# Delta-rule attention and a PReLU feed-forward on one core: order of transposes, fillers, copies and conversions around the opening

## The chip, the cores and the metric

The kernel runs on one core of a Trainium2 chip. The core has five engines that each work through their own instructions in order: TensorE (PE, matrix products, with a separate row PEld for loading the stationary operand), VectorE (DVE), ScalarE (ACT), GpSimd (POOL) and SyncE (SP, which here issues nearly all transfers). They wait for each other through semaphores. Products land in PSUM, from which DVE and ACT read. TensorE's clock is granted by a throttle, and the profile lists what was granted (1.00 is full speed, 0.50 half). The metric is the device time of one execution in microseconds, as a median over runs.

## What is computed

```python
# attention: batch 4, heads 8, 768 tokens, head dimension 48
k_n = k / (norm(k) + 1e-6)
for t in range(S):
    y[:, :, t] = einsum('bhd,bhde->bhe', q[:, :, t], state)
    v_old = einsum('bhde,bhd->bhe', state, k_n[:, :, t])
    state = state + beta[t] * einsum('bhd,bhe->bhde', k_n[:, :, t], v[:, :, t] - v_old)
x = y.transpose(0, 2, 1, 3).reshape(3072, 384)
# feed-forward: 384 -> 2048 -> 384
h = x @ w_in
g = maximum(h, 0) + alpha * minimum(h, 0)
out = g @ w_out
```

Everything is float32. A token's state depends on all tokens before it; within a chunk of tokens this dependence is a triangular system that can be solved at once.

## The kernel before

**Tiling.** The sequence is cut into 12 chunks of C = 64 tokens. A step `n` is one chunk for two of the four batches, so there are 24 steps; the partitions hold two times 64 tokens. In each step the inverse of a 64x64 triangular matrix per head is wanted. It is put together from 32x32 blocks (HB = 32): the two diagonal blocks are inverted, and the block between them follows from products (`between_1`, `between_2`).

**Inverting the diagonal blocks.** `grams(n)` multiplies keys with keys on PE, and DVE writes the scaled products to `same` (first columns) and `right` (second columns). `keep(n)` (line 424) copies the second half's own blocks, of 32 partitions and 256 elements each, from `right` to `same`: two copies a step, by DVE for n < 4 and t = 0 (line 430), otherwise by ACT (line 432). Four steps (NJ = 4) make one group m. After the fourth, DVE transposes the group to `block` (`turn_in`, 32x32 stream transposes, line 444), so that 128 blocks lie one in each partition. `eliminate(m)` inverts them there by 30 rounds of a product and a sum (lines 468 and 474). `back(m)` (line 480) transposes the result to two tiles, `turned` and `inverse`, in PIECES = 4 instructions each, first all of `turned`, then all of `inverse`. For the first group this takes too long, so `eliminate_small(0)` inverts only 16x16 blocks (14 rounds) and also ends in `back`; `cross` (line 527) joins them on PE: it multiplies `edge` with the first 16 rows or columns of `turned` (line 533), ACT copies the product to `half_way` (line 537), PE multiplies this with `inverse` (lines 542 and 548), and DVE adds it to `turned` (line 554) and `inverse` (line 556). These are 32x32x16 products.

**The opening.** The order of all instructions is written out by hand; an engine's instructions run in the order in which the code emits them. The first steps 0 and 1 are computed by `first_chunk` (line 1036). `place(i, (x,))` lets ACT copy parts of `turned` and `inverse` to `diag` and `inv` (line 579). `scale_v` scales v on DVE (line 643). `solve`, `outputs`, `next_state` and `to_ffn` are the products with the inverse (671), with the query products (684), for the new state (700), and transposes of the result (713); ACT copies the outputs to `y` (689) and to `xt` (715). `queries` (line 1017) multiplies the keys and queries of steps 0 and 1 ahead of time into a PSUM tile; its `mask(n)` lets DVE multiply them with a triangular mask into `a_t` (line 1029). `busy(n)` (line 967) issues `n` products of 128x128 with 128x512 whose result nobody reads: fillers (line 972).

**PSUM.** A tile `p_big` has two banks of 512 numbers a partition, and three buffers used in rotation; `ps_one` takes the first bank of one. Two more banks, `ffn_banks`, are used in turn by `ps_ffn`. The query products lie in a `p_big`, the fillers go to `ffn_banks`.

**Weights.** Both weight matrices are converted piece by piece (`weights`): a transfer brings a piece to a staging place, `begin` runs two ACT instructions on it (lines 205 and 206), and `finish`, a generator of two parts for each piece, runs two on DVE (lines 215 and 220), then lets SP fetch a further piece to the place that has come free (line 189). `part(gen, n)` takes n parts of a generator. w_in has 12 pieces and 6 places; its places lie in the tile of w_out. `begin_in(n)` makes sure that ACT has begun n pieces. `convert(n)` in `first_chunk` takes n parts of w_in's conversion; all in all it takes n = 14. w_out has 16 pieces (32 parts) and 7 places.

**The weaves.** `weave(*gens)` interleaves generators in proportion to the counts given with them. Four stages follow the opening:

- weave B: the second half of `cross(0)`, steps 2 and 3 (`ready`, `pair`), the rest of w_in's conversion with 10 parts of w_out's, `grams` of steps 4 to 7 (`statics`), and `ffn_in(0)`, the first product of the feed-forward for chunk 0 (PE line 802, ACT line 812, DVE line 814);
- weave C: the rest of w_out's conversion (22 parts), `ffn_in(1)`, `grams` of steps 8 and 9, and the first 12 parts of `eliminate(1)`;
- weave D: the other parts of `eliminate(1)` and `ffn_out(0)`, the second product (line 844), in which f runs over w_out's 16 row blocks, two products for each;
- after it, weave by weave, steps 4 to 23 with the feed-forward of the chunks before them.

Of the kernel before, what the change touches and what calls it, by code (L numbers as in the profile page):

```python
# [28 lines left out]
ALU = mybir.AluOpType  # L29
# [12 lines left out]
def kernel(  # L42
# [29 lines left out]
    def ps_big():  # L72


        return psum.tile([128, 2, 512], FP32, name="p_big", tag="big", bufs=3)
# [7 lines left out]
    def ps_ffn():  # L83
        turn[0] ^= 1
        return ffn_banks[turn[0]]

    def half(i):
        return slice(64 * i, 64 * i + 64)

    def dims(i):  # L90
        return slice(64 * i, 64 * i + D)
# [332 lines left out]
    def keep(n):  # L424

        m, j = n // NJ, n % NJ
        for t in range(2):
            own = slice(64 * t + HB, 64 * t + C)
            if n < NJ and t == 0:
                nc.vector.tensor_copy(out=same[m][own, j], in_=right[n % EARLY][own, 1:])  # L430
            else:
                nc.scalar.copy(same[m][own, j], right[n % EARLY][own, 1:])  # L432
        if j == NJ - 1 and m <= 2:
            for _ in turn_in(m):
                pass
# [3 lines left out]
    def turns(dst, src):  # L439


        n = HB // PIECES
        for i in range(PIECES):
            nc.vector.transpose(dst(slice(n * i, n * i + n)), src(slice(n * i, n * i + n)))  # L444
            yield
# [10 lines left out]
    def eliminate(m):  # L456

        if m > 2:
            yield from turn_in(m)
        r = block[m]  # L460
        nc.vector.tensor_tensor(out=r, in0=r, in1=inside, op=ALU.mult)
        nc.vector.memset(r.rearrange("p r c -> p (r c)")[:, :: HB + 1], 1.0)
        yield
        for j in range(1, HB - 1):
            n = HB - 1 - j
            prod = work.tile([128, HB * HB // 4], FP32, name="prod", bufs=2)
            prod = prod[:, 0 : j * n].rearrange("p (c i) -> p c i", c=j)
            nc.vector.tensor_tensor(  # L468
                out=prod,
                in0=r[:, 0:j, j : j + 1].to_broadcast([128, j, n]),  # L470
                in1=r[:, j : j + 1, j + 1 : HB].to_broadcast([128, j, n]),
                op=ALU.mult,
            )
            nc.vector.tensor_tensor(  # L474
                out=r[:, 0:j, j + 1 : HB], in0=r[:, 0:j, j + 1 : HB], in1=prod, op=ALU.add
            )
            yield
        yield from back(m)

    def back(m):  # L480
        r = block[m]
        turned[m] = work.tile([128, NJ * H, HB], FP32, name="turned", bufs=1)
        yield from turns(
            lambda x: turned[m][:, :, x].rearrange("c b r -> c r b"), lambda x: r[:, x]
        )
        inverse[m] = work.tile([128, NJ * H, HB], FP32, name="inverse", bufs=1)
        yield from turns(
            lambda x: inverse[m][:, :, x].rearrange("r b c -> r c b"),
            lambda x: r[:, :, x].rearrange("b r c -> b c r"),
        )  # L490

    WHOLE = HB - 1 + 2 * PIECES

# [2 lines left out]
    def eliminate_small(m):  # L496
        x = small[m]
        nc.vector.tensor_tensor(out=x, in0=x, in1=own_blocks(inside_), op=ALU.mult)
        nc.vector.memset(block[m][:, 0:LB, LB:HB], 0.0)
        nc.vector.memset(block[m][:, LB:HB, 0:LB], 0.0)  # L500
        nc.vector.memset(block[m].rearrange("p r c -> p (r c)")[:, :: HB + 1], 1.0)
        yield
        for j in range(1, LB - 1):
            n = LB - 1 - j
            prod = work.tile([128, HB * HB // 4], FP32, name="prod", bufs=2)
            prod = prod[:, 0 : 2 * j * n].rearrange("p (s c i) -> p s c i", s=2, c=j)
            nc.vector.tensor_tensor(
                out=prod,
                in0=x[:, :, 0:j, j : j + 1].to_broadcast([128, 2, j, n]),
                in1=x[:, :, j : j + 1, j + 1 : LB].to_broadcast([128, 2, j, n]),  # L510
                op=ALU.mult,
            )
            nc.vector.tensor_tensor(
                out=x[:, :, 0:j, j + 1 : LB], in0=x[:, :, 0:j, j + 1 : LB], in1=prod, op=ALU.add
            )
            yield
        yield from back(m)

    def edges(m, dst):

# [119 lines left out]
    def scale_v(n):  # L640
        if n < N and n not in nv:
            nv[n] = v_raw.pop(n)
            nc.vector.tensor_tensor(
                out=nv[n], in0=nv[n],
                in1=stats[n][0][:, :, None].to_broadcast([128, H, D]), op=ALU.mult,
            )
# [185 lines left out]
    def ffn_out(c, together=False):  # L832

        gs = gss.pop(c)
        p_o = {}
        if together:
            order = [(u, f) for f in range(FT) for u in range(2)]
        else:
            order = [(u, f) for u in range(2) for f in range(FT)]
        for u, f in order:  # L840
            assert len(out_done) > f
            if f == 0:
                p_o[u] = ps_ffn()[:, 0:DM]
            nc.tensor.matmul(  # L844
                p_o[u], gs[f // 2][:, f % 2, u * 128 : (u + 1) * 128], w_out[:, f],
                start=(f == 0), stop=(f == FT - 1),
            )
            if f == FT - 1:
                o_sb = work.tile([128, DM], FP32, name="o_sb")
                nc.scalar.copy(o_sb, p_o[u])  # L850
                store(c, u, o_sb)
            yield
# [67 lines left out]
    def part(gen, n):  # L920
        for _ in range(n):
            next(gen, None)
            yield

    def weave(*gens):

        live = [[0.0, i, 1.0 / n, g] for i, (g, n) in enumerate(gens)]
        while live:
            live.sort(key=lambda x: (x[0], x[1]))
            at = live[0]  # L930
            at[0] += at[2]
            try:
                next(at[3])
            except StopIteration:
                live.pop(0)
# [30 lines left out]

    def busy(n):

        if n > 0:
            p = ps_ffn()  # L970
            for _ in range(n):
                nc.tensor.matmul(p, ident, k_t[NJ - 1].rearrange("p g i -> p (g i)"))

    def pair(n):

# [40 lines left out]

    def queries():

        p = ps_big().rearrange("p a (n g i) -> p a n g i", n=2, g=G)
        for n in range(2):  # L1020
            for g, a, t in quarters():
                nc.tensor.matmul(
                    p[half(t ^ a), a, n, g], k_t[n][dims(a), g, half(t)],
                    q_t[n][dims(a), g, half(t)],
                )
            a_t[n] = work.tile([128, H, C], FP32, name="a_t")

        def mask(n):
            nc.vector.tensor_tensor(
                out=a_t[n].rearrange("p (a g) i -> p a g i", a=2), in0=p[:, :, n],  # L1030
                in1=minus[:, None, None, :].to_broadcast([128, 2, G, C]), op=ALU.mult,
            )

        return mask

    def first_chunk(mask, convert):

        both = (0, 1)
        middle = cross(0, slice(0, 2 * H), edge, half_way)
        next(middle)  # L1040
        busy(1)
        for i in both:
            mask(i)
        begin_in(6)
        convert(2)
        next(middle)
        busy(1)
        for i in both:
            place(i, (0,))
            scale_v(i)  # L1050
        for i in both:
            between_1(i)
            place(i, (1,))
        convert(4)
        busy(1)
        for i in both:
            place(i, (2,))
            between_2(i)
        begin_in(8)
        for i in both:  # L1060
            through_state(i)
        solve(0)
        convert(1)
        solve(1)
        convert(1)
        busy(1)
        for i in both:
            outputs(i)
            next_state(i)
            convert(2)  # L1070
            load_late(i + 2)
            load_v(i + 3)
        busy(1)
        for i in both:
            to_ffn(i)
        convert(2)
# [74 lines left out]
    begin_in(4)  # L1151
    for _ in eliminate_small(0):
        pass
    n = 14

    def convert(n):
        for _ in part(conv_in, n):
            pass
# [8 lines left out]
        (statics(NJ, 2 * NJ - 1), 2 * NJ + 1), (ffn_in(0), IN_PARTS),  # L1167
    )
    fetch_out(len(stages))
    blocks, SOON = eliminate(1), 12  # L1170
    weave(
        (conv_out, PARTS_OUT - 10), (ffn_in(1), IN_PARTS),
        (statics(2 * NJ, FIRST + 3), 2 * (FIRST + 4 - 2 * NJ) + 1), (part(blocks, SOON), SOON),
    )
    flips(FIRST + NJ, NJ)
# [1 line left out]
    prep(FIRST + NJ)  # L1177
    load_early(FIRST + NJ + NKE)
    load_q(NJ + 2)
    weave((part(blocks, WHOLE - SOON), WHOLE - SOON), (ffn_out(0, True), OUT_PARTS))  # L1180

    def prelude(n):
        place(n)
# [83 lines left out]
```

## Time and profile before

| | |
|---|---|
| median of 7 runs | 697.67 us (692.77 to 699.21) |
| the profiled execution | 696.54 us, its span 694.5 us |
| mean granted clock of PE | 0.988 |
| busy: PE, DVE, ACT | 671.5, 447.4, 253.0 us |
| weave B (54.1 to 102.0), busy PE / DVE / ACT | 46.19 / 30.90 / 31.55 of 47.9 us |
| weave C (102 to 134), busy PE / DVE / ACT | 26.13 / 26.14 / 20.67 of 32 us |
| weave D (134 to 154), busy PE / DVE / ACT | 20.00 / 17.47 / 0.89 of 20 us |
| from 200 us to the end, busy PE | 489.75 of 494 us |
| filler product, L972 | 26 records of two a product, 0.43 us apart at full clock |
| copy of own blocks by DVE (L430), by ACT (L432) | 0.28, 0.40 us |

How to read it: a time in the timeline counts from the first instruction of the span. A product in float32 leaves two records on PE. "L802" is line 802. In brackets behind an instruction stands the idle time of its engine before it, and the engine and line that ended it. The profiled execution is one of several; its clock, and with it its time, is its own.

### The profile page before, as it was taken

Reading aid. Unit: us, or ns where it says so; the run is one execution under the profiler, and the core shown is the slowest. Engines: PE = TensorE matmul, PEld = TensorE weight load, DVE = VectorE, ACT = ScalarE, POOL = GpSimd, SP = SyncE. Lnnn points to the kernel's source line nnn. Section 1 sums busy time; section 2 is a strip of 40 time slices with the busy share of each in tenths; the row PEclk is TensorE's granted clock in tenths of the full one; section 3 lists DMA queues with packets and bytes.
Section 4 is the critical chain, followed back from the end, with each engine's and each line's share of the span. In section 5 each row is a group of like instructions: output and inputs, shape, how many; then the busy total and the mean of one; then the engine's idle time right before and its main releaser. Section 6 shows DMA issues by size and latency. Waiting matters only on the chain.

```text
span 694.5 us, 22886 instructions
## 1 busy us (share of the span) xinstructions
PE 671.5 (97%) x10057; PEld 580.8 (84%) x10057; DVE 447.4 (64%) x1094; ACT 253.0 (36%) x603; POOL 19.5 (3%) x74
## 2 busy tenths in 40 slices
PE   6999998799999999999999999999999999999997
PEld 4577877556678998998998988988988989989997
DVE  5945778887898548957558967458867245245151
ACT  5836766415453243244243244124034034131020
POOL 4000001000000000000000000000000000000000
PEclk9969999999999999999999999999999999999999
DMA  8857653301322022022021111101111201100000
GB/s 130 221 145 183 156 114 111 76 10 40 62 57 48 13 59 48 13 59 47 14 59 37 35 26 36 37 24 36 36 27 35 47 21 30 33 4 2 24 1 23
DMA packets 110963, 37.76 MB, mean 54 GB/s; under 512 B 104160, under 2 KB 107248, under 8 KB 110864
## 3 DMA queue, kind: packets, MB, share of 16 engines
q1 hardware_dynamic: 109088, 35.81, 23.7%
q8 instruction: 79, 1.29, 0.8%
q10 hardware_dynamic: 1776, 0.49, 0.4%
q14 instruction: 20, 0.16, 0.1%
HBM read 31.56 MB, written 4.72 MB: 52 GB/s over the span
## 4 chain that ended last, share of the span: by engine, by line
PE 82%; DVE 9%; ACT 4%; DMA 2%; issue 1%; SPq 0%; ACTq 0%; DVEq 0%
PE p_ffn L802 32%; PE p_ffn L866 27%; PE p_ffn L844 4%; PE p_big L657 3%; PE p_big L384 3%; PE p_big L351 2%; PE p_big L614 2%; PE p_big L629 2%; PE p_big L671 2%; PE p_big L684 2%; PE p_big L700 1%; DVE prod L468 1%; DVE block L474 1%; DVE block L444 1%; PE p_big L713 1%
## 5 line engine op out<-in xcount | busy, mean ns | idle before, releaser
L802 PE MATMUL p_ffn<-xt,w_in 128*128 128x256 f32 x1152 | 268.8, 386 | 5.7 <-DVE sums L814 3.3
L802 PEld LDWEIGHTS p_ffn<-xt,w_in 128*128 128x128 f32 x1152 | 213.8, 191 | 36.9 <-ACT w_out L205 3.0
L814 DVE SCALAR_TENSOR_TENSOR act<-act,al_t,p_ffn 128x256 f32<-128x256 f32 x176 | 76.5, 476 | 71.7 <-ACT act L812 70.6
L812 ACT ACTIVATE act<-p_ffn 128x512 f32<-128x512 f32 x88 | 52.3, 594 | 120.4 <-PE p_ffn L802 120.3
L866 PE MATMUL p_ffn<-w_out,act 128*128 128x192 f32 x480 | 83.7, 328 | 0.0
L866 PEld LDWEIGHTS p_ffn<-w_out,act 128*128 128x128 f32 x480 | 78.6, 190 | 0.9
L474 DVE TENSOR_TENSOR block<-block,prod 128x30 f32<-128x30 f32 (+9 forms) x150 | 49.8, 332 | 5.2
L468 DVE TENSOR_TENSOR prod<-block 128x30 f32<-128x30 f32 (+9 forms) x150 | 48.8, 325 | 2.2
L886 DVE TENSOR_TENSOR o_sb<-u,p_ffn 128x192 f32<-128x192 f32 x40 | 13.3, 352 | 42.1 <-PE p_ffn L866 35.9
L373 ACT COPY q_t<-p_big 128x512 f32<-128x512 f32 x24 | 13.9, 590 | 58.0 <-PE p_big L351 58.0
L432 ACT COPY same<-right 32x256 f32<-32x256 f32 x44 | 17.7, 402 | 47.6 <-DVE right L393 47.4
L665 ACT COPY y<-p_big 128x384 f32<-128x384 f32 x22 | 10.5, 478 | 66.3 <-DVE r L660 66.3
L373 ACT COPY k_t<-p_big 128x512 f32<-128x512 f32 x24 | 13.9, 579 | 54.7 <-PE p_big L351 54.7
L866 PE MATMUL p_ffn<-space_out,sums 128*128 128x192 f32 x160 | 29.3, 326 | 0.0
L866 PE MATMUL p_ffn<-more,sums 128*128 128x192 f32 x160 | 29.3, 326 | 0.0
L866 PE MATMUL p_ffn<-w_out,sums 128*128 128x192 f32 x160 | 27.7, 326 | 0.0
L866 PEld LDWEIGHTS p_ffn<-more,sums 128*128 128x128 f32 x160 | 26.6, 190 | 0.0
L866 PEld LDWEIGHTS p_ffn<-space_out,sums 128*128 128x128 f32 x160 | 26.6, 190 | 0.0
L886 DVE TENSOR_TENSOR u<-u,p_ffn 128x192 f32<-128x192 f32 x20 | 7.0, 352 | 29.3 <-PE p_ffn L866 29.3
L866 PEld LDWEIGHTS p_ffn<-w_out,sums 128*128 128x128 f32 x160 | 25.8, 190 | 0.0
L579 ACT ACTIVATE diag<-inverse,which 64x128 f32<-64x128 f32 (+2 forms) x62 | 25.4, 412 | 0.9
L844 PE MATMUL p_ffn<-w_out,act 128*128 128x384 f32 x64 | 21.1, 489 | 2.2 <-DVE more L814 1.8
(150 smaller groups left out, 944.0 us busy)
## 6 DMA issues: line engine op xcount, KB each, us to landing
w_out<-in_moe_w_in_dram SPq DMA_DIRECT2D x12, 512.0 KB, 5.0
qp<-in_q_dram SPq DMA_DIRECT2D x48, 96.0 KB, 3.1
v_raw<-in_v_dram SPq DMA_DIRECT2D x48, 96.0 KB, 2.9
kl<-in_k_dram SPq DMA_DIRECT2D x96, 48.0 KB, 2.5
out_dram<-o_sb SPq DMA_DIRECT2D x92, 48.0 KB, 1.7
space_out<-in_moe_w_out_dram SPq DMA_DIRECT2D x11, 384.0 KB, 4.1
ke<-in_k_dram SPq DMA_DIRECT2D x43, 96.0 KB, 3.1
w_out<-in_moe_w_out_dram SPq DMA_DIRECT2D x5, 384.0 KB, 3.1
```

Source lines behind the costliest of these rows:

```text
L373: nc.scalar.copy(dst.rearrange("p g i -> p (g i)"), src)
L384: nc.tensor.matmul(p[half(t ^ a if w else t), a, w, g], k_t[n][dims(a), g, half(t)], rhs[n][dims(a), g, half(t)],)
L468: nc.vector.tensor_tensor(out=prod, in0=r[:, 0:j, j : j + 1].to_broadcast([128, j, n]), in1=r[:, j : j + 1, j + 1 : HB].to_broadcast([128, ...
L474: nc.vector.tensor_tensor(out=r[:, 0:j, j + 1 : HB], in0=r[:, 0:j, j + 1 : HB], in1=prod, op=ALU.add)
L579: nc.scalar.mul(dst[n % NE][to or rows, a.start * G : a.stop * G, cols], src[m][rows, heads], which[rows, i : i + 1],)
L657: nc.tensor.matmul(p[half(t), a, w, g], x[n][dims(a), g, half(t)], state[bp][dims(a), t, g])
L802: nc.tensor.matmul(p_h[:, i], w_in[:, t, (f + i) * 128 : (f + i + 1) * 128], xt[:, t], start=(t == 0), stop=(t == KT - 1),)
L812: nc.scalar.activation(g, p_h, ACT.Relu, scale=-1.0)
L814: nc.vector.scalar_tensor_tensor(out=g[:, i], in0=g[:, i], scalar=al_t[:, f + i : f + i + 1], in1=p_h[:, i], op0=ALU.mult, op1=ALU.add,)
L844: nc.tensor.matmul(p_o[u], gs[f // 2][:, f % 2, u * 128 : (u + 1) * 128], w_out[:, f], start=(f == 0), stop=(f == FT - 1),)
L866: nc.tensor.matmul(p, x(i), w(i), start=(i == 0), stop=(i == FP - 1))
L886: nc.vector.tensor_tensor(out=to, in0=x, in1=p, op=ALU.add)
```

## The change

- `back(m, late)`: for the first group (`eliminate_small`), two pieces of `turned` are transposed, then the four of `inverse`, then the other two of `turned`.
- `queries` writes its products to the two `ffn_banks`, one for each `a`; `mask(n)` becomes two DVE instructions of half the size. `busy(n)` writes to a `p_big`, and takes fractions: 1.5 is one product of 512 columns and one of 256.
- `first_chunk`: the masks come after the first `place`; the first `convert(2)` is gone (12 parts instead of 14 are converted in the opening, so weave B gets two more); `scale_v(0)` comes before, `scale_v(1)` after; the filler before `place` is 1.5 instead of 1.
- `keep(n)`: for n = 4 to 9 both copies are made by DVE.
- weaves C and D: the last 6 parts of w_out's conversion move from C to D, where their proportion is 16 against 32 for `ffn_out(0)`; in C `ffn_in(1)` has a proportion of 44 for its 48 parts.

```diff
-            if n < NJ and t == 0:
+            if (n < NJ and t == 0) or NJ <= n < FIRST + NJ:
                 nc.vector.tensor_copy(out=same[m][own, j], in_=right[n % EARLY][own, 1:])
...
-    def back(m):
+    def back(m, late=False):
+
         r = block[m]
         turned[m] = work.tile([128, NJ * H, HB], FP32, name="turned", bufs=1)
-        yield from turns(
+        transposed = turns(
             lambda x: turned[m][:, :, x].rearrange("c b r -> c r b"), lambda x: r[:, x]
         )
+        for _ in range(PIECES // 2 if late else PIECES):
+            next(transposed)
+            yield
         inverse[m] = work.tile([128, NJ * H, HB], FP32, name="inverse", bufs=1)
         yield from turns(
...
+        yield from transposed
...
-        yield from back(m)
+        yield from back(m, True)
...
     def busy(n):
-        if n > 0:
-            p = ps_ffn()
-            for _ in range(n):
-                nc.tensor.matmul(p, ident, k_t[NJ - 1].rearrange("p g i -> p (g i)"))
+        p = ps_one()
+        while n > 0:
+            x = p[:, 0 : int(512 * min(n, 1))]
+            nc.tensor.matmul(
+                x, ident, k_t[NJ - 1].rearrange("p g i -> p (g i)")[:, 0 : x.shape[-1]]
+            )
+            n -= 1
...
     def queries():
-        p = ps_big().rearrange("p a (n g i) -> p a n g i", n=2, g=G)
+        p = [x.rearrange("p (n g i) -> p n g i", n=2, g=G) for x in ffn_banks]
...
         def mask(n):
-            nc.vector.tensor_tensor(
-                out=a_t[n].rearrange("p (a g) i -> p a g i", a=2), in0=p[:, :, n],
-                in1=minus[:, None, None, :].to_broadcast([128, 2, G, C]), op=ALU.mult,
-            )
+            for a in range(2):
+                nc.vector.tensor_tensor(
+                    out=a_t[n][:, a * G : (a + 1) * G], in0=p[a][:, n],
+                    in1=minus[:, None, :].to_broadcast([128, G, C]), op=ALU.mult,
+                )
...
         next(middle)
         busy(1)
-        for i in both:
+        begin_in(6)
+        scale_v(0)
+        next(middle)
+        busy(1.5)
+        for i in both:
+            place(i, (0,))
             mask(i)
-        begin_in(6)
-        convert(2)
-        next(middle)
-        busy(1)
-        for i in both:
-            place(i, (0,))
-            scale_v(i)
+        scale_v(1)
         for i in both:
             between_1(i)
...
-    n = 14
+    n = 12
...
-    blocks, SOON = eliminate(1), 12
+    blocks, SOON, LAST = eliminate(1), 12, 6
     weave(
-        (conv_out, PARTS_OUT - 10), (ffn_in(1), IN_PARTS),
+        (part(conv_out, PARTS_OUT - 10 - LAST), PARTS_OUT - 10 - LAST), (ffn_in(1), IN_PARTS - 4),
         (statics(2 * NJ, FIRST + 3), 2 * (FIRST + 4 - 2 * NJ) + 1), (part(blocks, SOON), SOON),
     )
...
-    weave((part(blocks, WHOLE - SOON), WHOLE - SOON), (ffn_out(0, True), OUT_PARTS))
+    weave(
+        (conv_out, OUT_PARTS // 2), (part(blocks, WHOLE - SOON), WHOLE - SOON),
+        (ffn_out(0, True), OUT_PARTS),
+    )
```

## The prediction

> **What bounds the kernel now.** I read the page's busy shares and slices first. TensorE (PE) is busy 97% of the 694.5 us, but the row of the granted clock has one slice far below full:
>
> ```profile
> PE 671.5 (97%) x10057; PEld 580.8 (84%) x10057; DVE 447.4 (64%) x1094; ACT 253.0 (36%) x603; POOL 19.5 (3%) x74
> ...
> PEclk9969999999999999999999999999999999999999
> ```
>
> From about 200 us on PE is full at full clock (489.75 of 494 us) and none of that code changes, so what the change is worth is decided before about 155 us and then shifts the end. Four stages lie there: the opening (to 54.1 us, where the second `cross` begins), weave B (54.1 to 102: `ffn_in(0)`), weave C (102 to 133.9: `ffn_in(1)`), weave D (133.9 to 154: `ffn_out(0)`).
>
> Second, busy time by stretch. The clock rises at 23.0 and changes in steps of 3.41 us, so I cut the opening there. Columns: stretch, length, busy time of each engine, clock, DMA share, GB/s.
>
> ```profile
> 29.82:33.24 3.42, 2.95 (x152) 2.04 (x144) 3.42 (x8) 2.83 (x6) 0.00 (x0) 1.00 0.53 91
> 33.24:36.65 3.41, 2.48 (x135) 1.52 (x122) 2.29 (x6) 1.08 (x3) 0.00 (x0) 1.00 0.62 116
> 36.65:40.06 3.41, 3.41 (x64) 3.41 (x64) 2.83 (x6) 1.11 (x3) 0.00 (x0) 0.50 0.75 196
> 40.06:43.48 3.42, 3.42 (x30) 1.85 (x30) 0.00 (x0) 2.79 (x6) 0.00 (x0) 0.50 0.77 256
> 43.48:46.89 3.41, 3.41 (x92) 3.41 (x94) 0.96 (x3) 1.34 (x2) 0.00 (x0) 0.50 0.12 47
> 46.89:50.30 3.41, 3.41 (x62) 1.82 (x54) 1.90 (x4) 0.00 (x0) 0.00 (x0) 0.50 0.19 34
> ...
> 57.13:60.54 3.41, 3.21 (x197) 2.72 (x195) 1.77 (x4) 3.14 (x8) 0.74 (x2) 1.00 0.61 110
> 60.54:63.96 3.42, 3.42 (x8) 2.42 (x8) 2.38 (x6) 1.08 (x3) 0.00 (x0) 0.50 0.74 192
> ```
>
> See two falls to half: 13.65 us from 36.65, and one step from 60.54. The steps before both hold mainly the 32x32 products of `cross` (L542, L548). In the chain of waits 36.6 to 54.1 is nearly all PE, with fillers (L972) on it, so half clock there costs time.
>
> Third, the timeline, where the chain turns and PE stops:
>
> ```profile
> 27.88 2.01 DVE L444 STREAM_TRANSPOSE turned<-block 128x256 f32<-128x256 f32 x4
> 29.73 2.21 DVE L444 STREAM_TRANSPOSE inverse<-block 128x256 f32<-128x256 f32 x4
> ...
> 43.98 0.67 ACT L205 ACTIVATE w_in<-w_out 128x512 uint32<-128x512 uint32 x1 [0.85 <-DMA w_out<-in_moe_w_in_dram]
> ...
> 120.76 0.82 ACT L432 COPY same<-right 32x256 f32<-32x256 f32 x2 [2.97 <-DVE right L393]
> ...
> 123.25 1.53 PE L802 MATMUL p_ffn<-xt,w_in 128*128 128x256 f32 x6 [2.61 <-DVE sums L814]
> ...
> 133.91 20.23 PE L844 MATMUL p_ffn<-w_out,act 128*128 128x384 f32 x62 [1.82 <-DVE more L814]
> ```
>
> Weave B is bound by PE (46.19 of 47.9 us). Weave C is not: PE and VectorE (DVE) are busy 26.1 of 32 us each, and PE stops for products that DVE and ScalarE (ACT) finish late.
>
> **Part 1, the transposes.** The first half of `turned` ends at 28.97, as now, so L533 still starts at 29.13. The four `inverse` pieces then run 28.8 to 31.0 instead of 29.7 to 31.94, and L542 waits for the half_way copy (ACT, to 31.17) and the filler's issue (to 31.4): start 31.45 for 32.09, **-0.64**. The other two `turned` pieces fall to DVE while PE works; `place` reads them much later.
>
> **Part 2, fillers, masks, order.** With the queries in the two ffn banks, their mask no longer has to come early. The 1.27 us of masks and convert(2) leave DVE's idle stretch before the adds (L554, L556) and come after them. Four masks of 128x256 replace two of 128x512: at the 0.35 spacing of L393's like rows 1.4 us, +0.2, beside PE work (DVE then idles 4.67 us ahead of L635). L548 ends 34.5, the adds 35.4, the ACT copy 35.95: L614 starts at 36.0 for 36.63. The filler of 1.5 takes 1.28 us (0.427 a product in the first fillers) and just fits between.
>
> The question is the clock. The Trainium skill, "TensorE: Matmul & The Clock Gate", section "Why this matters for your kernels", says the clock goes to half after an idle window, and returns once TensorE has been busy some 4 us. By that rule nothing here should have fallen: PE was busy 2.48 of 3.41 us before 36.65, its longest gap 0.48; and with PE busy 3.41 of 3.41 it should have come back at 40.06. It stayed at 0.50 for three more steps. By the rule part 2 brings only the 0.64 already counted; by the rows dense products count and small ones hardly do. The step kept at full clock (29.82) and the step that fell (33.24) both hold one filler (0.855 us, 25%), so the limit lies close to that, and half a filler more (37%) keeps the clock in a step that holds it. I follow the rows. Then, at full clock: L614 36.0 to 38.05 (half of the 3.63 and a little), filler to 38.9, L629 to 41.0, L671 to 42.2 with DVE's L675 between, filler to 43.05, first L684/L700 to 44.1.
>
> Here a **new wait** comes. convert(2) also sent w_in's piece 6 (SP queue, 35.88). Now the first conversion runs after the masks and scale_v(1), done about 38.8, the second 39.8. A piece lands about 5.46 us after the conversion that frees its place (L220 ended 38.49, ACT could begin 43.98): 44.2 and 45.3. ACT meets begin_in(8) already at 39.9 and is in order, so the y copies behind it (L689) run at 46.8, after two beginnings of 1.28. p_big has three buffers in rotation, so the second L700 waits for the first y copy; behind it stand a filler, L713 and the second `cross`. That puts L533 at 49.5 with the clock full, for 54.12: -4.6. But PE then idles 44.6 to 47.35, and the step 43.48 to 46.89 holds no dense product, like that before 60.54. I take that row: one step at half, +1.5: L533 at 51.0, **-3.1** in all with part 1. Bounds: -0.64 (clock falls as before) to -7.2 (no wait and no fall). On SP, load_late(2) waits behind piece 9's place, not piece 10's: earlier, not later.
>
> **Part 3, copies of own blocks.** For n = 4 to 9 twelve copies leave ACT (0.40, L432) and come to DVE (0.28, L430): ACT -4.8, DVE +3.4. In B eight are beside PE work. PE's one stop there (0.96 at 101.61, for the xt copy that stood behind two L432) should go: **-1.0**. The step with the small products before 60.54 recurs: 0 (bounds -1.7, +1.7 for one step's half). B also takes two conversion parts (1.1 us of DVE, 64% busy there): 0.
>
> **Part 4, last conversions into D.** C loses three pieces: DVE about 0.75 each (0.35 and 0.56, overlapping), ACT 1.06 each. With n = 8, 9 of part 3: ACT -3.2 and -1.6, DVE -2.3 and +1.1. PE's stops in C are 0.71, 0.33, 2.61, 0.40 and 1.82 = 5.9 us. The last goes, since the last four ffn_in parts now run with no conversion before their L814: -1.8. Of the 2.61 at least the 0.82 of L432 go and part of DVE's backlog: -1.2. The two small ones: -0.3. Sum **-3.3**. Bounds: 0 (the DMA that ACT waited 1.43 for at 115.14 still sets the pace) and -5.9 (PE's own work, about 25.2 of 32, plus little).
>
> In D the 2.3 us of conversion come on top of DVE's 18.5 us (134.86 to 153.3). PE has 20.2. DVE then ends some 2 us after PE's last L844; the first L614, 2.5 us after that product now, needs DVE's end and one ACT copy (0.5): late by about 0.2. **+0.3**; the whole 2.3 if that slack is not there. w_out's last pieces are needed 80% through D and are converted in its first 60%.
>
> **Sum**: -3.1 - 1.0 - 3.3 + 0.3 = -7.1 on the profiled execution. It took 696.54 (span 694.5 and 2.04 around it), 1.13 below the median of the runs shown, 697.67. I take the median as base: 697.67 - 7.1 = 690.6, of which I give **690.3** as half the clock's steps can fall kinder.
>
> **Rivals.** (a) The clock falls in the opening as before: the fillers sit elsewhere relative to the 3.41 us steps. For: one filler was just too little; between 31.4 and 34.5 there is still only small work. Against: half a filler more. Then -0.64 - 1.0 - 3.3 + 0.3: 693.0. (b) C keeps its pace because w_out's transfers set it (ACT's 1.43 wait, SP's 25.8 us of waits on L220); only the opening is won: 697.67 - 3.4 = 694.3. (c) Slower: DVE becomes the bound from 60 to 155. It takes 3.4 us of copies, 1.1 of conversion in B, 2.3 in D, 0.2 of masks = 7.0; if each is met on the path and ACT's relief frees nothing, only the opening's 3.1 comes off: 701.6. It decides once DVE has no idle left under PE's work; in 100 to 110 it is already busy 9.74 of 10, against it stand 64% in B and 1 us less of work in C.
>
> **Numbers.** Forecast 0.53, (a) 0.22, (b) 0.14, (c) 0.11. The forecast's own range is 686 to 694, by the opening's and C's bounds. Low end of the 8 in 10: nearly all won, -7.2 - 1.7 - 4.5 = -13.4: 684.3; high end past (b): 695.5. A measurement of this kernel tells about 0.5%, 3.5 us, from no change. Faster: 0.53 nearly whole, seven tenths of (a), half of (b): 0.75; slower: (c) and little else: 0.10; same 0.15.
>
> **What would show it.** L542 near 31.4 and full clock in the step after it; the y copies behind w_in's seventh and eighth beginnings, with PE idle before the second L700; L844 with no wait for L814; DVE's transposes in D ending after PE's last L844. It is wrong if the clock is at half for over 10 us before 55 us, if PE waits for DVE throughout B, or if weave C stays near 32 us.

## The result, and the profile after

The changed kernel takes 692.29 us as a median of 22 runs (686.28 to 696.77); the kernel before took 696.94 beside it (57 runs). The ratio is 0.9931, with a 95% interval of 0.9914 to 0.9948: 4.8 us less. Forecast were 690.3 us and -7.1. Sign and range hold; a third of the gain is missing.

One caution for every time below: the profiled execution of the changed kernel is the slowest of its 22 (696.77, span 695.0), so it is read for what happens in it, stage by stage, and the total comes from the medians.

The page of the changed kernel, its busy shares, clock slices and the row of one transfer queue (packets, MB, share):

```profile
PE 670.4 (96%) x10059; PEld 580.3 (84%) x10059; DVE 450.5 (65%) x1108; ACT 249.1 (36%) x591; POOL 19.2 (3%) x74
...
PEclk9998999999999999999999999999999999999999
...
q8 instruction: 79, 1.29, 0.8%
```

The slice at 6 tenths is gone from the clock. The queue row will matter: 79 packets of together 1.29 MB, 16,384 bytes each. TensorE has 20,118 products and loads here, some 255 for each packet.

Busy time by stretch, cut at the clock's steps, same columns as in the prediction:

```profile
31.97:35.38 3.41, 2.19 (x145) 1.77 (x146) 0.26 (x1) 2.22 (x4) 0.00 (x0) 1.00 0.67 124
35.38:38.79 3.41, 3.41 (x73) 1.93 (x61) 2.46 (x7) 0.91 (x2) 0.00 (x0) 0.50 0.20 35
38.79:42.21 3.42, 3.42 (x75) 2.47 (x74) 2.64 (x6) 1.94 (x6) 0.00 (x0) 1.00 0.12 34
...
49.03:52.45 3.42, 2.57 (x83) 1.51 (x78) 3.14 (x7) 0.93 (x3) 0.00 (x0) 1.00 0.68 213
52.45:55.86 3.41, 0.42 (x49) 0.33 (x41) 0.00 (x0) 0.07 (x1) 0.00 (x0) 1.00 0.59 109
55.86:59.27 3.41, 3.41 (x55) 3.01 (x52) 1.77 (x4) 2.47 (x7) 0.53 (x1) 0.50 0.82 218
...
62.69:66.10 3.41, 1.20 (x6) 0.73 (x4) 3.18 (x8) 0.99 (x2) 0.00 (x0) 1.00 0.98 336
66.10:69.51 3.41, 2.75 (x11) 2.47 (x12) 0.00 (x0) 0.64 (x2) 0.00 (x0) 0.50 0.51 121
```

The opening has one step at half clock (from 35.38) where the kernel before had four. But two stretches appear in which PE hardly works: 0.42 of 3.41 us after 52.45, with DVE and ACT idle too, and 1.20 after 62.69. Half clock follows both: one step from 55.86 and two from 66.10, 10.2 us, where the kernel before had one step in weave B. Up to 80 us it is 13.7 us at half clock for 17.1, so two thirds of the 10.2 us that the opening saved come back there. The timeline says what ended them (lines are shifted by some five: `cross` is L538, L547, L553; fillers L977; `ffn_in` L807 and L819; `ffn_out` L849):

```profile
27.79 1.09 DVE L444 STREAM_TRANSPOSE turned<-block 128x256 f32<-128x256 f32 x2
28.73 2.17 DVE L444 STREAM_TRANSPOSE inverse<-block 128x256 f32<-128x256 f32 x4
30.81 1.03 DVE L444 STREAM_TRANSPOSE turned<-block 128x256 f32<-128x256 f32 x2
...
44.89 0.69 ACT L205 ACTIVATE w_in<-w_out 128x512 uint32<-128x512 uint32 x1 [2.27 <-DMA w_out<-in_moe_w_in_dram]
...
47.73 0.46 ACT L694 COPY y<-p_big 128x384 f32<-128x384 f32 x1
...
51.88 0.88 PE L538 MATMUL p_big<-turned,sums 32*32 32x16 f32 x82
55.74 0.78 PE L538 MATMUL p_big<-turned,sums 32*32 32x16 f32 x46 [2.99 <-issue]
...
66.76 1.22 PE L807 MATMUL p_ffn<-xt,w_in 128*128 128x256 f32 x2 [2.87 <-issue]
...
104.77 1.89 PE L807 MATMUL p_ffn<-xt,w_in 128*128 128x256 f32 x8
...
113.81 2.83 PE L807 MATMUL p_ffn<-xt,w_in 128*128 128x256 f32 x12 [1.43 <-DVE sums L819]
...
132.82 20.81 PE L849 MATMUL p_ffn<-w_out,act 128*128 128x384 f32 x64
...
159.47 0.71 PE L634 MATMUL p_big<-diag,mid 64*64 64x32 f32 x18 [0.80 <-ACT mid L624]
```

In the kernel before, the second `cross` ran in one piece:

```profile
54.12 1.38 PE L533 MATMUL p_big<-turned,sums 32*32 32x16 f32 x128
```

Now it starts at 51.88. After 82 of its 128 records it stands for 2.99 us, in the middle of one unbroken series, and the releaser is "issue": the profile shows nothing that PE waited for. The same happens inside `ffn_in(0)`, 2.87 us. The chain of waits has it on the path (start, length, what):

```profile
51.10 0.85 PE p_big L718 x6
51.95 0.81 PE p_big L538 x63
52.76 2.99 issue
55.74 0.78 PE p_big L538 x46
```

Stage by stage, in profiled executions (us from the start of the span):

| kernel | second `cross` | `ffn_in(0)` | transposes for `xt`, steps 2 and 3 | `ffn_out(0)` ends | span |
|---|---|---|---|---|---|
| before | 54.12 | 55.93 | 98.53 | 154.1 | 694.5 |
| changed | 51.88 | 57.36 | 104.11 | 153.6 | 695.0 |
| opening's edits alone | 50.85 | 56.32 | 101.28 | 157.7 | 698.2 |
| copies alone | 55.11 | 57.09 | 101.94 | 156.7 | 697.1 |
| conversions alone | 56.30 | 58.11 | 98.52 | 149.0 | 689.5 |
| changed, short transfers | 50.48 | 52.57 | 93.55 | 143.0 | 684.4 |

The changed kernel is 2.2 us ahead at the second `cross`, 1.4 behind when `ffn_in(0)` begins, 5.6 behind when weave B ends, and then wins 6.1 in weaves C and D. These are single executions; the parts are compared by medians below.

### The profile page after: what moved, and what is told of

It reads as the page before. It is cut to its first block, busy times and chain, and to the rows that moved or that the text cites. A ratio compares the mean times of both kernels' runs of the same rounds, so it can differ in the third digit from the quotient of the medians.

```text
span 695.0 us, 22895 instructions
## 1 busy us (share of the span) xinstructions
PE 670.4 (96%) x10059; PEld 580.3 (84%) x10059; DVE 450.5 (65%) x1108; ACT 249.1 (36%) x591; POOL 19.2 (3%) x74
## 3 DMA queue, kind: packets, MB, share of 16 engines
q8 instruction: 79, 1.29, 0.8%
## 4 chain that ended last, share of the span: by engine, by line
PE 84%; DVE 9%; ACT 3%; issue 2%; DMA 1%; ACTq 0%; SPq 0%; DVEq 0%
PE p_ffn L807 35%; PE p_ffn L871 27%; PE p_big L662 3%; PE p_big L384 3%; PE p_big L351 3%; PE p_big L977 2%; PE p_big L689 2%; PE p_big L676 2%; DVE prod L468 2%; DVE block L474 2%; PE p_big L619 2%; PE p_big L634 2%; PE p_big L705 1%; DMA ke<-in_k_dram 1%; PE p_big L718 1%
## 5 line engine op out<-in xcount | busy, mean ns | idle before, releaser
L807 PE MATMUL p_ffn<-xt,w_in 128*128 128x256 f32 x1152 | 269.6, 387 | 5.7 <-issue 2.9
L807 PEld LDWEIGHTS p_ffn<-xt,w_in 128*128 128x128 f32 x1152 | 214.8, 192 | 36.7 <-issue 6.0
L819 DVE SCALAR_TENSOR_TENSOR act<-act,al_t,p_ffn 128x256 f32<-128x256 f32 x176 | 76.4, 475 | 68.6 <-ACT act L817 67.5
L327 DVE TENSOR_REDUCE norm<-ksq 128x8 f32<-128x384 f32 x24 | 12.9, 546 | 20.4 <-ACT ksq L325 20.4
L871 PEld LDWEIGHTS p_ffn<-w_out,sums 128*128 128x128 f32 x160 | 25.8, 190 | 0.0
L432 ACT COPY same<-right 32x256 f32<-32x256 f32 x32 | 12.9, 402 | 34.6 <-DVE right L393 34.4
```

Of the source, the lines that this page charges most:

```text
L807: nc.tensor.matmul(p_h[:, i], w_in[:, t, (f + i) * 128 : (f + i + 1) * 128], xt[:, t], start=(t == 0), stop=(t == KT - 1),)
L819: nc.vector.scalar_tensor_tensor(out=g[:, i], in0=g[:, i], scalar=al_t[:, f + i : f + i + 1], in1=p_h[:, i], op0=ALU.mult, op1=ALU.add,)
L871: nc.tensor.matmul(p, x(i), w(i), start=(i == 0), stop=(i == FP - 1))
```

## The experiments

Ratios are to the kernel before on the same chip, with 95% intervals; "x us" is the ratio's difference from 1 times some 698 us.

### One part at a time

Theory: the parts bring what the prediction's sum says. Rivals: the opening's gain is eaten by a stop, or the weaves' gain isn't there.

The opening's edits alone: `back(m, True)`, query products and fillers with exchanged banks, the new order in `first_chunk`, 12 parts for 14.

> The kernel before with the opening's edits alone (late second half of turned, query products and fillers swapped, new order of first_chunk, 12 parts); own copies and weaves C and D as before. Theory 1 (the sum of the prediction): -3.1 us, some 693.8; the clock holds through the step after L547 in most executions. Theory 2 (PE's instruction supply: in the profile after, PE stood 1.22, 2.99 and 2.87 us marked 'issue' in or behind the 32x32 products, before only 0.48 and some 0.5): what the clock gives is lost to such gaps, within 1.5 us of before, and the profile shows issue gaps of over 2 us before 70 us.

Ratio 1.0001 (0.9975 to 1.0026): nothing. Its timeline has the forecast in its first line and the reason in the next two:

```profile
50.85 0.88 PE L538 MATMUL p_big<-turned,sums 32*32 32x16 f32 x82
54.71 0.77 PE L538 MATMUL p_big<-turned,sums 32*32 32x16 f32 x46 [2.99 <-issue]
...
65.46 1.22 PE L807 MATMUL p_ffn<-xt,w_in 128*128 128x256 f32 x2 [2.59 <-issue]
```

Second `cross` at 50.85, where 51.0 was forecast, 3.3 us ahead of before; then 2.99 us of "issue" give nearly all of it back.

The copies alone:

```diff
-            if n < NJ and t == 0:
+            if (n < NJ and t == 0) or NJ <= n < FIRST + NJ:
```

> The kernel before with the own copies of n = 4 to 9 on VectorE alone. Theory 1: the stop at 101.6 us for xt goes (-1.0) and 0.8 of the stop before L802 in weave C: -1.8 us, some 695.1. Rival (VectorE becomes the bound): its 3.4 us more show as up to +3.4. Third: no change, since PE's work hides both.

0.9982 (0.9959 to 1.0004), -1.3 us; the interval reaches 0.

The conversions alone (the edits of weaves C and D, with the proportion 44):

> The kernel before with the last six parts of w_out's conversion moved from weave C to D alone. Theory 1: the stop before the first L844 goes (-1.8) and the conversions' share of the other stops (-0.4), weave D costs +0.3: -1.9 us. Theory 3 (weave C held more than the stops named: in the profile after, the stretch from the transposes L713 of steps 2 and 3 to the first product of ffn_out(0) is 28.7 us for 35.4): -3 us or more. Rival: weave D grows by the whole 2.3 us and nothing is won: 0 to +0.4.

0.9921 (0.9904 to 0.9938), **-5.5 us**: as much as the whole change. All stops of PE in weave C with their releasers:

```profile
107.90 2.83 PE L802 MATMUL p_ffn<-xt,w_in 128*128 128x256 f32 x12 [0.41 <-ACT space_out L206]
...
120.59 5.67 PE L802 MATMUL p_ffn<-xt,w_in 128*128 128x256 f32 x24 [0.21 <-ACT space_out L206]
...
128.76 20.23 PE L844 MATMUL p_ffn<-w_out,act 128*128 128x384 f32 x62 [0.37 <-ACT q_t L373]
```

Before they were 0.71, 0.33, 2.61, 0.40 and 1.82 us, 5.9 in all; now 1.0. From the transposes for `xt` (98.5 in both) to the L844 that waits, 35.4 us have become 30.2. The 2.61 in the middle of C went whole, without a copy having moved: the conversions' backlog was enough to make it.

The late half of the transposes alone:

> The kernel before with the second half of turned transposed last, alone. Theory 1: L542 0.64 us earlier, -0.6 us, which a measurement hardly tells from no change. Theory 2: the products L542 and L548 then start nearer to the end of the instruction supply, the gap marked issue inside them grows from 0.48 by about what was won, and L614 starts no earlier than 36.5 us.

0.9984 (0.9965 to 1.0003), -1.1 us, where -0.64 was forecast; not told from 0.

The proportion 44 for `ffn_in(1)` alone, with the conversions left in C:

> The kernel before with ffn_in(1) at a proportion of 44 for its 48 parts in weave C, all conversions left in C. If the conversions moved out are what e3 won by (-5.5 us), this alone gives 0 to -1 us (the last L814 no longer stand behind conversions: part of the 1.82 us before the second L844). If the pace is what won, -3 us or more.

0.9993 (0.9965 to 1.0022), -0.5 us. The pace by itself is not told from 0; what wins is that the conversions leave.

### What "issue" is

I counted TensorE's records from the start of the program (loads, products and semaphore instructions together). In all fourteen profiles of this case, every "issue" stop of over 0.3 us stands within three records of instruction 961, 1217, 1473, 1729, 1985, 2241 or 2497: always 705 plus a multiple of 256. One packet of 16,384 bytes on the queue of instructions ends 1.2 to 1.7 us before PE goes on. So the theory: PE's program arrives in blocks of 256 instructions, and a stop is a block that came late. A 32x32 product of `cross` uses up four instructions (two records of a load, two of a product), so its 64 products are exactly one block, gone in under 2 us.

At 1985 the order decides. In all seven profiles with the old order PE passes it without such a stop; in the five with the new order and whole transfers (the shifted kernel at the end of this section set aside) it stands for 2.99, 2.99, 2.03, 1.89 and 2.42 us. At 2497 both orders stop in some profiles: the old one for up to 3.04 us (copies alone), the new one for 0.30 to 2.88. The length depends on the execution too: up to instruction 961, TensorE's program is the same in the kernel before and in those with copies, conversions, pace, or conversions and copies alone, and the stop there was 0.48, 2.02, 1.20, 1.38 and 0.43 us. So a difference of 1 us between two single profiles says little.

Why late? The next two kernels shorten a transfer: of w_in's pieces 6 to 11 they bring only the first 128 of 1024 words (so half of w_in isn't what the reference has). The weights arrive as 64-bit numbers, which is why a 128x512 piece is 512 KB; the float32 of the computation is made on the chip.

```diff
-                nc.sync.dma_start(out=words(i)[0], in_=pieces[i][1].bitcast(U32))
+                to, of = words(i)[0], pieces[i][1].bitcast(U32)
+                if count == 12 and i >= 6:
+                    to, of = to[:, 0:128], of[:, 0:128]
+                nc.sync.dma_start(out=to, in_=of)
```

In the changed kernel:

> The changed kernel, but w_in's pieces 6 to 11 bring only the first 128 of 1024 words of a row, so that their columns are wrong; every instruction stays. PE takes its instructions in blocks of 256: all its stops marked 'issue' after the change lie at the 961st, 1985th or 2497th instruction. Theory 2 (a block is asked for when the one before is entered, and its 16,384-byte packet waits for w_in's transfers): the packets before 2.4 us after the crossing, the stops at 1985 and 2497 shrink from 2.99 and 2.87 to under 0.6 us, and the time falls by 4 to 6 us below the changed kernel, to some 686 to 688. Rival (the blocks are too short for the small products whatever the transfers do): the stops stay at 2.5 to 3 us, and only ScalarE's wait of 2.27 us for piece 6 goes, -1.5 us at most.

and in the kernel before:

> The kernel before with the same shortened pieces. Theory 2: it has stops of only 0.48 and 0.44 us at block borders and ScalarE waits 0.85 us for piece 7 beside PE's work, so it gains 0 to 1.5 us, much less than the changed kernel does. Rival (w_in's transfers hold up both kernels alike): it gains as much as the changed kernel, 3 us or more.

The changed kernel falls to 0.9874 (0.9841 to 0.9907), -8.8 us, against -4.8 without this edit; the kernel before to 0.9983 (0.9957 to 1.0009), -1.2. Short transfers are worth 4.0 (give or take 2.6) to the new order and 1.2 (give or take 1.8) to the old; that they are worth more to the new one is likely, but the two are not told apart (2.8, give or take 3.2). The first of the two in the timeline:

```profile
50.48 0.88 PE L541 MATMUL p_big<-turned,sums 32*32 32x16 f32 x82
51.58 0.57 PE L541 MATMUL p_big<-turned,sums 32*32 32x16 f32 x46 [0.23 <-issue]
...
59.31 0.59 PE L810 MATMUL p_ffn<-xt,w_in 128*128 128x256 f32 x2 [0.76 <-issue]
```

Same place, record 82, and 0.23 us for 2.99; at 2497 0.76 for 2.87. With the stops small, PE's clock stays full from 38.9 us almost to the end.

The prediction had another candidate, ACT's new wait for w_in's seventh piece (2.27 us in the timeline above). Here four parts of the conversion run early, in DVE's idle time ahead of the adds (two did in the kernel before), so that the piece is there in time; all in all the opening takes 14 parts again:

```diff
         begin_in(6)
+        convert(4)
         scale_v(0)
...
-            convert(2)
             load_late(i + 2)
...
-        convert(2)
+        convert(4)
```

> The changed kernel with four parts of w_in's conversion put into VectorE's idle 3 to 4 us ahead of the adds, and those of the outputs' loop moved behind to_ffn (14 parts in the opening). The places of pieces 0 to 3 come free earlier, so pieces 6 to 9 travel at 33 to 46 us, ScalarE no longer waits for piece 6, and fewer transfers stand before the packet that is asked for near 47 us. Theory 2: the second L538 run starts at 49 us or earlier and its stop shrinks below 1.5 us; -2 to -4 us against the changed kernel, some 688 to 690. Rival (stops stay, or move to the next block): within 1 us of the changed kernel.

0.9931 (0.9905 to 0.9957), the changed kernel's own ratio. The first copy of `y` comes at 46.13 instead of 47.73, and the second `cross` starts at 50.84, as with the wait (50.85 in the opening alone). **The new wait costs nothing**: PE's last stop before it is for DVE's `state` (0.70 us) in both. The stop at instruction 1985 is 2.03 us, where under 1.5 was expected.

Next, everything that moves data is taken out of the stretch before that block: w_in's conversions partly early and partly at the end (14 parts; the two beside the `solve` calls are moved too), the loads of k and v behind the transposes for `xt`.

```diff
+        convert(4)
         scale_v(0)
...
         for i in both:
             outputs(i)
             next_state(i)
-            convert(2)
-            load_late(i + 2)
-            load_v(i + 3)
...
-        convert(2)
+        convert(6)
+        for i in both:
+            load_late(i + 2)
+            load_v(i + 3)
```

> The changed kernel with w_in's conversions arranged so that hardly a transfer is under way when PE crosses into its 1729th instruction near 47 us: four parts in VectorE's idle time ahead of the adds, four after the masks, the other six and the loads of k and v behind to_ffn. Theory 2: the packet starts within 1.5 us of the crossing, the stop at 1985 falls from 2.99 us to under 0.5; the later stop at 2497 may stay, since the transfers moved out then run at 50 to 60 us. Some -2 us against the changed kernel if the later stops don't grow, within 1 us if they take it back. Rival (the stop at 1985 does not hang on transfers that are under way): it stays above 2 us.

0.9923 (0.9891 to 0.9956). The stop at 1985 was to go, and it is still 1.89 us. The stretch from where PE enters block 1729 to where the next packet begins, by busy time:

```profile
46.18:49.83 3.65, 2.80 (x55) 1.71 (x58) 2.69 (x6) 0.79 (x2) 0.00 (x0) 1.00 0.06 10
```

The transfers' share is 0.06 (10 GB/s), and the packet came 3.65 us after that entry all the same. In this execution, bytes in flight were not what held it; nor were newly issued transfers at first, for SyncE issued none between 40.37 and 48.76.

The stop at 2497 shrank to 0.30 us here, and the transposes for `xt` begin at 95.62, 8.5 us before those of the changed kernel. But this profile is the fastest of the kernel's 7 executions (687.86), and the median is 692.93, no better than the changed kernel's. Whether the other executions have longer stops or lose the time elsewhere is not shown.

The table has what I counted from the records: when PE entered the block before, when the packet came, and the stop.

| kernel | PE enters the block at 1729 | packet for 1985 | stop at 1985 |
|---|---|---|---|
| before | 51.18 | 52.14 to 53.12 | none |
| opening alone | 47.29 | 52.24 to 53.12 | 2.99 |
| changed | 48.32 | 52.84 to 54.17 | 2.99 |
| short transfers | 48.03 | 49.17 to 50.12 | 0.23 |
| four parts early | 47.29 | 51.58 to 52.46 | 2.03 |
| moved transfers | 46.18 | 49.83 to 51.28 | 1.89 |
| old filler (below) | 46.38 | 50.75 to 51.81 | 2.42 |

The packet follows by 1.0 us (before) or 1.1 (short transfers), or by 3.7 to 5.0 in the others.

A last kernel tests the block theory without touching any transfer: 30 small products more, 120 instructions, ahead of the first query products.

```diff
     def queries():
+        for _ in range(30):
+            nc.tensor.matmul(ffn_banks[0][0:HB, 0:LB], ident[0:HB, 0:HB], ident[0:HB, 0:LB])
```

> The changed kernel with 30 products of 32x32x16 more (60 records of a product and 60 of a load, 120 instructions) ahead of the first query products, where TensorE stood idle 0.60 us for the transposed queries; nothing else moves. Theory (TensorE's instructions arrive in blocks of 256, and a stop marked 'issue' stands where a block ends): the blocks' borders are counted from the start of the program, so every stop moves 120 instructions ahead in the code. The stop of 2.99 us that stood after 82 of the 128 records of the second first-half product of cross (L538) now stands after some 82 - 60 = 22 of them, and the one that stood after 6 of 8 records of ffn_in (L807, at 66.8) moves into the 32x32 products before it (L553, after some 70 of 126 records). Their length stays 2 to 3 us, and the time within 0.5% of the changed kernel's (0.993 of before). Rival (something at that place in the program stops TensorE: an operand, a bank, or a transfer that the profile doesn't name): the stops stay after record 82 of L538 and ahead of the same products of L807, wherever the borders are.

```profile
56.45 0.37 PE L538 MATMUL p_big<-turned,sums 32*32 32x16 f32 x22
57.37 1.20 PE L538 MATMUL p_big<-turned,sums 32*32 32x16 f32 x106 [0.55 <-issue]
...
61.95 0.88 PE L553 MATMUL p_big<-inverse,act 32*32 32x16 f32 x71
67.29 0.94 PE L553 MATMUL p_big<-inverse,act 32*32 32x16 f32 x54 [4.47 <-issue]
```

Record 22 for the forecast 22, and 71 for some 70: the stops are tied to the count, not to the place in the program. So they are the ends of blocks. Their lengths were not as forecast (0.55 and 4.47, not 2 to 3), and neither was the time: 1.0027 (0.9997 to 1.0058), not 0.993. The 30 products took 3.38 us at half clock, where 0.60 us were idle, and the whole opening moved by 2.2; the first `cross` has two stops (1.37 and 1.50) for one of 1.22. What else makes up the 6.7 us between the two kernels' ratios I did not trace.

### Filler and combination

The changed kernel with the old filler, `busy(1)` for `busy(1.5)`:

> The changed kernel with one filler instead of one and a half ahead of place. If the half filler is what shortens the spell of half clock (one step of 3.41 us in the profiles with the changed opening, 13.65 to 17.07 in those with the old one), the spell is 10 us or longer again, and the second L538 run starts at 54 us or later. Rival (the new order alone does it, the products then stand closer together): one step again, and PE reaches L538 within 0.5 us of the 50.9 us of e1.

0.9921 (0.9889 to 0.9952), no worse than the change. Its busy time by stretch, around the place of that filler:

```profile
33.85:37.26 3.41, 2.80 (x98) 1.84 (x87) 2.65 (x8) 0.99 (x3) 0.00 (x0) 1.00 0.53 98
37.26:40.67 3.41, 3.13 (x70) 2.32 (x70) 2.46 (x5) 2.27 (x6) 0.00 (x0) 1.00 0.16 43
```

The clock stays full through the opening, from 23.55 to 54.27, without the half filler. Its stops are 2.42 us at 1985 and 2.73 at 2497, as in the changed kernel, and this profile (692.73) is its median execution.

The opening of before with the conversions and the copies of the change:

> The changed kernel with the opening of before: moved conversions and own copies on VectorE. If the two add up (-5.5 and -1.3 alone), some 691.0, ratio 0.990. If the copies only take the slack that the conversions leave (VectorE enters weave D later, and the chain behind it grows by the 1.0 us that the changed kernel shows there), the ratio is that of e3, 0.992, or up to 0.9935.

0.9898 (0.9861 to 0.9935), -7.1 us, a median of 691.4 over 9 runs (683.86 to 693.42). It beats the kernel before; against the changed kernel (0.9914 to 0.9948) the intervals overlap, so it is not shown to be better. The two parts alone add to -6.8, so their sum stands without the new opening.

## Why the prediction was right, and where it was wrong

**Part 1, transposes:** the step happened. The `inverse` pieces run from 28.73 to 30.9 (forecast 28.8 to 31.0). Its 0.64 can't be told from 0 in the total.

**Part 2, the clock:** the cold spell shrank from 13.65 to 3.41 us, but my reason was wrong. I set the rows against the rule of the Trainium skill ("TensorE: Matmul & The Clock Gate", "Why this matters for your kernels") and concluded that half a filler more would keep the clock. With one filler it kept it too. What decides is the new order: all seven profiles with the old opening have 13.65 to 17.07 us at half clock in it, the six with the new one (the 30 products of the shift set aside) 0 to 3.42. Which part of the order does it was not tried. In the changed kernel the clock fell for one step, after a stretch with PE busy 2.19 of 3.41 us, its longest gap 1.22, and came back after one step of full work (35.38 to 38.79), as that rule has it; a fall at a gap of 1.22 is again not in the rule.

**Part 2, the new wait:** it came where the prediction put it (ACT 2.27 us, `y` at 47.73 for 46.8), and it cost nothing, where I charged 2.6 and 1.5. The second `cross` at 51.0 was nearly met (50.85 and 51.88), with other terms: L619 began at 38.95, not 36.0, because a stop of 1.22 and a filler of 2.8 us at half clock stood ahead of it.

**The step that failed** is the end of that part: "L533 at 51.0, **-3.1** in all". It let what is won at the start of the second `cross` come off the end, and put the supply of instructions at nothing. In place of that gain stands the stop inside those very products, 2.99 us. The old order hid it: PE reached instruction 1985 at 54.93, 1.8 us after the packet had ended. The opening's -3.1 became 0.0 (-1.7 to +1.8). The half clock behind the stops belongs to the same cost: with the opening alone, steps from 54.85 and 65.09. What the stops cost in the median is known only from the short transfers, which take 4.0 us (give or take 2.6) off the changed kernel.

**Part 3, copies:** -1.0 in B and 0.82 of the stop in C were forecast, -1.3 was measured. With the copies alone the stop of 2.61 shrinks to 1.74, by 0.87, but the first stop in C grows from 0.71 to 1.70 and takes it back. The stop for `xt` (0.96) is gone (L807 at 104.77 has none); with the conversions alone it stays, 0.97.

**Part 4, conversions:** the mechanism was right and its size too small. The forecast split PE's stops in C into 1.8 for the tail, 1.2 of 2.61 and 0.3. All of the 2.61 went by the conversions alone: they are worth -5.5, near the bound of -5.9 that the prediction had named. The term that was too small is the 1.2 for this stop. Rival (b), that w_out's transfers set C's pace, falls: with the conversions alone ACT's wait of 1.43 for a transfer went with the stops. (Its 25.8 us of SyncE's waits are those of the whole run; in C they are 15.9. And its -3.4 does not follow from the parts, where the opening alone is -3.1.) Rival (c) does too: DVE is busy 29.72 of the 32 us between 102 and 134 in the changed kernel (26.14 before), and PE still works 30.28 of them.

**Weave D:** +0.3 was forecast. From its end to the end of the span takes 541.4 us in the changed kernel and in every other with conversions and copies together, 540.6 with the conversions alone, 540.4 before: +1.0. L634 waits 0.80 for ACT's `mid`.

By parts, then: 0.0, -1.3 and -5.5 instead of the forecast's -3.1, -1.8 and -2.5 (C's -3.3 without the copies' 0.82; the D term set aside), against -4.8 for the whole; the total was near because two errors, a missing cost and a gain sized too small, had opposite signs. That it came within 2 us of the forecast is luck; that weave C would bring a gain is not.

Open: what delays a block's packet. For instruction 1985 and with the new order it came early in the one profile with short w_in pieces, and late in the five with whole ones, even where hardly any bytes moved. What in those transfers holds it was not found.

## What to carry to other kernels

In these profiles a stretch of very small products eats a block of 256 instructions in 1.4 to 2 us, faster than the next one arrived at any stop (even with short transfers it took 3.55 us, from 48.03 to 51.58, from entering one block to using the next). Before a gain is booked on such a stretch, count its instructions and ask what hid the supply until now. An unexplained "issue" in the middle of an unbroken series is the sign; the test is that its place moves when instructions are added far ahead. And where an engine's backlog makes a stop, take the whole stop as the bound of what relief is worth, not the share of the instructions that are moved.

## What the hardware showed that was not expected

- TensorE's instructions come by transfer, 16,384 bytes for 256 of them, mostly 0.9 to 1.5 us each, and a late one stops PE for up to 4.47 us (in the shifted kernel).
- A stop can cost more than its length: in the profiles with the new order, half clock begins during or at most 1.6 us behind every stop of over 1.8 us at 1985 or 2497.
- The profile can put such a stop down to something else: before, a stop ahead of `ffn_in` at 64.15 was ascribed to a load of keys, 0.55 us; it stands at instruction 2497, and its packet ended at 63.12, 1.58 us before PE went on. With the old filler the stop of 2.73 us there is ascribed to a load of w_out, and its packet ended 1.44 us before.
- The clock: a stretch with PE busy 2.57 of 3.41 us kept full clock (49.03, changed kernel); in the kernel before one with 2.48 lost it (33.24), and one with 3.21, mainly of small products, lost it too (57.13). Busy time alone does not decide.
